# The causal mask and V's column sums go from TensorE to VectorE in a two-stage attention kernel

## The chip, the cores and the metric

The kernel runs on one core of a Trainium2 chip, as one program. The metric is the device time of one execution in microseconds (us). Several executions were timed, and one more was taken by the hardware profiler; the trace of that one is read below. The engines are PE (TensorE, matrix products), DVE (VectorE), ACT (ScalarE), POOL (GpSimd) and SP (SyncE, which issues the DMAs). PEld stands for the loading of PE's weights, the operand that stays in the array.

## The reference

Two stages. The first is attention of 8 heads in which a query sees only the keys that fall into the same hash bucket; the second is a mixture of 4 experts, each an attention with a causal mask, of which every token takes the best two.

```python
# first stage: batch 4, heads 8, sequence 768, head 64, 6 bits
q_bucket = np.sum((q @ proj > 0) * powers, axis=-1)      # k_bucket in the same way
mask = q_bucket[:, :, :, None] == k_bucket[:, :, None, :]
scores = np.where(mask, scale * q @ k.T, -1e9)
attn = softmax(scores)
x = attn @ v                                              # heads side by side: 512 columns

# second stage: 4 experts
logits = x @ w_gate                                       # the best two of four, softmax of these
scores = scale * (x @ wq[e]) @ (x @ wk[e]).T
scores = np.where(causal, -1e9, scores)                   # above the diagonal
out += gate * softmax(scores) @ (x @ wv[e]) @ wo[e]
```

(Shortened; `softmax` stands for the subtraction of the maximum, the exponential and the division.)

## The kernel before

**Units.** The work falls into 32 units of the first stage, ("L", batch, head), and 16 of the second, ("M", batch, expert). The list `seq` interleaves them: the experts of one batch stand between the heads of the next, and the last batch's experts come at the end. Heads are handled in pairs, and there are 16 pairs. The head with an even number is the first of its pair.

**A unit.** `max_steps` computes the scores once for their row maxima on DVE. `shift_steps` turns those into a row that is added through the product. `s_unit` then computes the scores a second time, transposed, in 6 chunks of 512 columns or fewer (`L_S`, `M_S`), in three steps for each chunk, `qk`, `lo` and `av`:

- `qk`: two matmuls of half-precision parts into one bank of PSUM (the accumulators that PE writes and DVE and ACT can read), then two exponentials on ACT, `p` in fp32 and `ph` in fp16. In an "M" unit a block on the diagonal gets a third matmul between the two, `ident16` against `mask_t`, which adds a large negative number above the diagonal. A unit has 6 such blocks, in 5 of its chunks.
- `lo`: POOL forms `pl`, the difference of `p` and `ph`.
- `av`: for each block of 128 queries and 128 keys three matmuls with `ph` or `pl` as the weights and 64 or 65 columns of `vh` or `vl` (V's high and low half) as the moving operand. The 65th column holds ones, so that the denominator comes along. `av` runs four to five chunks behind `qk`.

At the end of an "L" unit six matmuls of `vs` add a term with the sums of V's columns, and `normalise` divides.

**V.** `prep_v` prepares a pair: ACT writes V scaled as `vf` (fp32) and `vh` (fp16), POOL the difference `vl`. Each is one tile for the pair, with a column of ones at its outer sides: the first head's slice starts at element 1 and its denominator comes first (`first=1`, `den=0`), the second head's starts at element 66. Then PE sums V over all keys: 12 matmuls with one moving column (`ones`), which leave the sums as a column; a copy to `vcol`; a transpose on PE with `vcol` as weights; a copy and a subtraction to `vr`, two half-precision rows; and a DMA into `vs`:

```python
for n in range(2 * NT):
    x = vl[:, n // 2].rearrange("p h d -> p (h d)") if n % 2 else vh[:, n // 2, 2:2 + 2 * D]
    nc.tensor.matmul(p[:, 0:1], x, ones[:, 0:1], start=not n, stop=n == 2 * NT - 1)
```

**What sets the order.** Nothing is issued as it is written. A recorder (`Recorder`) collects every operation, and `schedule` lays them out on the engines, each engine in a fixed order. It goes by the table `TIMES` (what an operation costs by engine, operands and size), by a priority for each job (its place in the program plus the entry of the table `PLACE` for that job and engine), and by what is free: 8 PSUM banks, of which scores take up to 3 for `qk` (`st`), 2 for maxima (`mx`), 1 for the product with V (`o`) and 2 for the rest (`misc`). Copies out of PSUM may go to ACT or to DVE as the times fall (`copy`). In the first microseconds matmuls with `ident` fill PE's holes. Every operation has the one line L777 in the profile, where `issue` makes it, so names of tiles tell operations apart: `bank` is any bank of PSUM.

Of the kernel before, what the change touches and what calls it, by code (L numbers as in the profile page):

```python
# [134 lines left out]
class Op:  # L135
# [96 lines left out]
sync wo_l fr 768 773 701 1090 -400 0  # L232
gpsimd memset one - 2 1 SS 104 175 0 0 0
# [557 lines left out]
SHARED = 5  # L791
WHOLE = (4,)
# [26 lines left out]
def tile_kernel(ctx, tc, q, k, v, proj, wqk, wvg, wo, out):  # L819
# [71 lines left out]
    nc.gpsimd.memset(ones, 2.0 ** -10)  # L891

# [68 lines left out]
    FQ = [con.tile([128, S], HF, name=f"fq{i}") for i in range(2)]  # L961
    FQ.append(wo_l.rearrange("p t m -> p (t m)")[:, 0:S])
# [20 lines left out]
    for t in VR:  # L983
        nc.gpsimd.memset(t, 0.0)
        nc.gpsimd.memset(t[:, 0, 0:2], S / 1024.0)
        nc.gpsimd.memset(t[:, 0, 130:132], S / 1024.0)
    for t in VH + VF:
        nc.gpsimd.memset(t[:, :, 0:2], 1.0)
        nc.gpsimd.memset(t[:, :, 130:132], 1.0)
# [8 lines left out]
    wo_h = con.tile([128, EP, Dm], HF, name="wo_h")  # L998
# [286 lines left out]
    def prep_v(b, hp):  # L1285
# [13 lines left out]
        for h in range(2):  # L1299
            cv = vf[:, :, 2 + D * h:2 + D * h + D]  # L1300
            nc.scalar.activation(cv, nat[:, h].rearrange("p (j d) -> p j d", j=NT), AF.Copy, scale=c)
            hv = vh[:, :, 2 + D * h:2 + D * h + D]
            nc.scalar.activation(hv, cv, AF.Copy)
            nc.gpsimd.tensor_tensor(vl[:, :, h], cv, hv, op=OP.subtract)
            if not h:
                yield 0
        for h in range(2):
            w = slice(1 + 65 * h, 66 + 65 * h)
            U["L", b, 2 * hp + h].update(vf=vf[:, :, w], vh=vh[:, :, w], vl=vl[:, :, h], first=1 - h, den=64 * h,
                                         order=[2 * (i % 3) + i // 3 for i in range(NT)], c=c, vs=vs.rearrange("p h d -> p (h d)")[:, w])  # L1310
        yield 0
        p = misc()
        for n in range(2 * NT):
            x = vl[:, n // 2].rearrange("p h d -> p (h d)") if n % 2 else vh[:, n // 2, 2:2 + 2 * D]
            nc.tensor.matmul(p[:, 0:1], x, ones[:, 0:1], start=not n, stop=n == 2 * NT - 1)
        col = sb.tile([128, 1], FT, name="vcol")
        nc.copy(col, p[:, 0:1])
        nc.tensor.transpose(p[0:1, 128:256], col, ident)
        vr = VR[(npair[0] - 1) % NV]
        nc.copy(vr[:, 0, 2:2 + 2 * D], p[0:1, 128:256])  # L1320
# [116 lines left out]
    def s_unit(u):  # L1437
# [11 lines left out]
        def qk(c):  # L1449
            def f():  # L1450
                p = psum.tile([128, 512], FT, name="st", bufs=3)
                o = 0
                for j, q0, q1 in chunks[c]:
# [4 lines left out]
                    if diag:  # L1458
                        nc.tensor.matmul(p[:, o:o + 128], ident16, mask_t, start=False, stop=False)
# [514 lines left out]
```

## Time and profile before

| | us |
|---|---|
| median of 3 runs | 603.07 (602.51 to 603.36) |
| the profiled execution | 602.15 |
| its span, first to last instruction | 600.2 |
| PE busy | 587.3 (98%) |
| ACT busy | 502.4 (84%) |
| DVE busy | 493.3 (82%) |
| POOL busy | 471.3 (79%) |
| PE's weight loads busy | 429.2 (72%) |

The granted clock of PE is 0.998 of full speed over the span. Matmuls overlap: the time of one runs from its start to the modelled end of its result, while the next one starts long before that. What a matmul keeps PE from is read from start to start.

### The profile page before, as it was taken

How to read it: one execution, taken by the hardware profiler on the slowest of the kernel's cores; microseconds unless marked ns; L12 is line 12 of the kernel's file. 1: busy time of each engine (PE TensorE's matmuls, PEld its weight loads, DVE VectorE, ACT ScalarE, POOL GpSimd, SP SyncE). 2: the span in 40 equal slices, each digit the busy share in tenths (PEclk: the TensorE clock that was granted, in tenths of full speed). 3: DMA queues.
4: the chain of work that ended last, by engine and by line, in shares of the span. 5: the costliest groups of instructions: out<-in, count | busy, mean ns of one | idle time of the engine just before them, and what ended most of it. 6: DMA issues, size and time to landing. Idle time of an engine off the chain costs nothing.

```text
span 600.2 us, 20646 instructions
## 1 busy us (share of the span) xinstructions
PE 587.3 (98%) x7908; PEld 429.2 (72%) x7908; DVE 493.3 (82%) x1363; ACT 502.4 (84%) x1082; POOL 471.3 (79%) x527
## 2 busy tenths in 40 slices
PE   8999999999999999999999999999999999999996
PEld 7677776777777777777757676777667677767673
DVE  5998999999799898969868799987994886647843
ACT  6589999999799988897879897977879897954593
POOL 9479999898698998796967988977868797943291
PEclk9999999999999999999999999999999999999999
DMA  5563153241313223140341413240241111011212
GB/s 182 152 185 99 36 169 109 51 156 35 119 44 99 70 92 75 39 129 3 114 124 57 138 29 116 67 132 4 86 135 56 43 46 29 3 47 28 89 54 106
DMA packets 32920, 50.26 MB, mean 84 GB/s; under 512 B 6410, under 2 KB 20534, under 8 KB 32822
## 3 DMA queue, kind: packets, MB, share of 16 engines
q1 hardware_dynamic: 32810, 48.95, 28.1%
q8 instruction: 62, 1.02, 0.7%
q14 instruction: 36, 0.29, 0.2%
q10 hardware_dynamic: 12, 0.00, 0.0%
HBM read 20.98 MB, written 6.29 MB: 45 GB/s over the span
## 4 chain that ended last, share of the span: by engine, by line
PE 83%; ACT 7%; DVE 4%; issue 3%; POOL 2%; DMA 1%; POOLq 0%; ACTq 0%; DVEq 0%
PE bank L777 83%; ACT ph L777 3%; ACT p L777 2%; POOL pl L777 2%; DVE pmw L777 1%; DVE qk L777 1%; DMA xt<-roww 1%; ACT qk L777 0%; POOL vl L777 0%; DVE xt L777 0%; ACT vf L777 0%; DVE bank L777 0%; ACT wst L777 0%; DVE mw L777 0%; DVE pm L777 0%
## 5 line engine op out<-in xcount | busy, mean ns | idle before, releaser
L777 POOL TENSOR_TENSOR pl<-p,ph 128x512 f16<-128x512 f32 (+1 forms) x373 | 415.7, 1142 | 108.5 <-PE bank L777 57.4
L777 PE MATMUL bank<-qk 128*128 128x512 f16 (+13 forms) x1464 | 318.1, 323 | 0.7 <-DMA qk<-roww 0.5
L777 ACT ACTIVATE p<-bank 128x512 f32<-128x512 f32 x376 | 235.6, 632 | 22.4 <-PE bank L777 19.6
L777 ACT ACTIVATE ph<-bank 128x512 f16<-128x512 f32 x376 | 236.2, 637 | 2.8 <-PE bank L777 2.8
L777 DVE TENSOR_REDUCE pm<-bank 128x2 f32<-128x512 f32 (+2 forms) x284 | 184.1, 672 | 13.2 <-PE bank L777 12.7
L777 PEld LDWEIGHTS <-ph 128*128 128x128 f16 x2912 | 165.6, 98 | 25.9 <-issue 1.7
L777 PEld LDWEIGHTS <-qk 128*128 128x128 f16 (+5 forms) x1560 | 128.8, 98 | 47.4 <-issue 2.9
L777 PEld LDWEIGHTS <-pl 128*128 128x128 f16 x1456 | 134.9, 97 | 17.9 <-POOL pl L777 9.1
L777 PE MATMUL bank<-vh,pl 128*128 128x65 f16 x1120 | 135.7, 194 | 1.9 <-POOL pl L777 1.6
L777 PE MATMUL bank<-vl,ph 128*128 128x64 f16 x1120 | 136.3, 192 | 0.0
L777 PE MATMUL bank<-vh,ph 128*128 128x65 f16 x1120 | 136.1, 195 | 0.2
L777 PE MATMUL bank<-xt,wqk_h 128*128 128x384 f16 x256 | 56.0, 326 | 0.0
L777 DVE CUSTOM_DVE_ANT_0 spare<-bank,causal 128x512 bf16<-128x512 f32 (+2 forms) x96 | 44.1, 460 | 4.6 <-PE bank L777 2.9
L777 PE MATMUL bank<-mvh,pl 128*128 128x65 f16 x336 | 39.0, 193 | 0.5 <-POOL pl L777 0.4
L777 PE MATMUL bank<-mvh,ph 128*128 128x65 f16 x336 | 39.4, 194 | 0.0
L777 PE MATMUL bank<-mvl,ph 128*128 128x64 f16 x336 | 39.4, 192 | 0.0
L777 PEld LDWEIGHTS <-xt 128*128 128x128 f16 x324 | 30.2, 97 | 10.9 <-ACT xt L777 0.5
L777 PEld LDWEIGHTS <-wqk_h 128*128 128x128 f16 x256 | 24.1, 97 | 13.6 <-issue 0.3
L777 POOL TENSOR_TENSOR vl<-vf,vh 128x384 f16<-128x384 f32 x32 | 30.1, 951 | 3.6 <-ACT vh L777 1.7
L777 ACT ACTIVATE qk<-bank 128x384 f16<-128x384 f32 x29 | 14.2, 491 | 20.2 <-PE bank L777 19.8
L777 PE MATMUL bank<-wvg_h,xt 128*128 128x260 f16 x192 | 30.6, 274 | 0.0
L777 PE MATMUL bank<-xt,wqk_l 128*128 128x384 f16 x128 | 28.7, 326 | 0.0
(192 smaller groups left out, 862.1 us busy)
## 6 DMA issues: line engine op xcount, KB each, us to landing
qk<-qk SPq DMA_DIRECT2D x128, 96.0 KB
natv<-in_v_dram SPq DMA_DIRECT2D x16, 384.0 KB
qk<-qk SPq DMA_DIRECT2D x32, 192.0 KB
natq<-in_q_dram SPq DMA_DIRECT2D x15, 384.0 KB
natk<-in_k_dram SPq DMA_DIRECT2D x15, 384.0 KB
out_dram<-ot SPq DMA_DIRECT2D x20, 256.0 KB
wst<-in_wqk_dram SPq DMA_DIRECT2D x4, 256.0 KB
xt<-xt SPq DMA_DIRECT2D x4, 192.0 KB
```

Source lines behind the costliest of these rows:

```text
L777: o.made = getattr(getattr(self.nc, e), m)(*[real(x) for x in args], **{k: real(x) for k, x in kw.items()})
```

## The change

Five things.

- In batches three and four (`DMB = 2`) the mask matmul goes. In its place DVE adds `mask_t` to the diagonal blocks of the finished scores in PSUM, one instruction for a chunk, before the two exponentials. A chunk with two diagonal blocks gets one instruction over both.
- The sums of V: DVE reduces `vf` over the key blocks to `vsum`, and one fp32 matmul with a column of constants (`onef`) as weights gives the row of sums at once. The 12 matmuls, `vcol` and the transpose go.
- V's slices: in `vh`, `vf`, `vs` and `vr` the ones stand behind the first head's columns in place of before them. Slices start at elements 0 and 66, and `first` and `den` go.
- The three matmuls of a block in `av` are issued as `ph` with `vh`, `pl` with `vh`, `ph` with `vl`; before, the last two stood the other way round.
- `wo_h` (weights of the last product) is allocated earlier and lends its memory to one of the constant rows `FQ`, to make room. `PLACE` has new numbers throughout, and `TIMES` has entries for the new operations.

```diff
 PLACE = [
-    -2340, -66, -2158, -3742, 130, -1484, -2346, 0, -378, 2664, 594, -22, 1009, 7069, -1117, 0, -1213, 0, -496, -5437, 407, -4, -1918, 0,
...
+    -3968, -12221, -4294, 0, 0, -3011, 1476, -10216, -3028, 1347, 0, -672, -3509, -16, -851, -3, 291, -2773, -6556, 0, 25, 0, 0, 0,
...
+tensor matmul dt.float32 128 misc - 215 400 0 0 0
+vector tensor_reduce vsum vf 128 768 SS 870 950 0 0 0
...
+vector tensor_tensor st st 128 128 PP 235 260 0 0 0
+vector tensor_tensor st st 256 256 PP 370 395 0 0 0
...
+DMB = 2
...
+    onef = con.tile([128, 1], FT, name="onef")
+    nc.gpsimd.memset(onef, 2.0 ** -10)
...
-    FQ = [con.tile([128, S], HF, name=f"fq{i}") for i in range(2)]
-    FQ.append(wo_l.rearrange("p t m -> p (t m)")[:, 0:S])
+    wo_h = con.tile([128, EP, Dm], HF, name="wo_h")
+    FQ = [con.tile([128, S], HF, name="fq0")] + [x.rearrange("p t m -> p (t m)")[:, 0:S] for x in (wo_h, wo_l)]
...
     for t in VH + VF:
-        nc.gpsimd.memset(t[:, :, 0:2], 1.0)
+        nc.gpsimd.memset(t[:, :, D:D + 2], 1.0)
         nc.gpsimd.memset(t[:, :, 130:132], 1.0)
...
-            cv = vf[:, :, 2 + D * h:2 + D * h + D]
+            cv = vf[:, :, 66 * h:66 * h + D]
             nc.scalar.activation(cv, nat[:, h].rearrange("p (j d) -> p j d", j=NT), AF.Copy, scale=c)
-            hv = vh[:, :, 2 + D * h:2 + D * h + D]
+            hv = vh[:, :, 66 * h:66 * h + D]
...
-            w = slice(1 + 65 * h, 66 + 65 * h)
-            U["L", b, 2 * hp + h].update(vf=vf[:, :, w], vh=vh[:, :, w], vl=vl[:, :, h], first=1 - h, den=64 * h,
+            w = slice(66 * h, 66 * h + 65)
+            U["L", b, 2 * hp + h].update(vf=vf[:, :, w], vh=vh[:, :, w], vl=vl[:, :, h],
...
-        for n in range(2 * NT):
-            x = vl[:, n // 2].rearrange("p h d -> p (h d)") if n % 2 else vh[:, n // 2, 2:2 + 2 * D]
-            nc.tensor.matmul(p[:, 0:1], x, ones[:, 0:1], start=not n, stop=n == 2 * NT - 1)
-        col = sb.tile([128, 1], FT, name="vcol")
-        nc.copy(col, p[:, 0:1])
-        nc.tensor.transpose(p[0:1, 128:256], col, ident)
+        sums = sb.tile([128, 2, D], FT, name="vsum", bufs=1)
+        nc.vector.tensor_reduce(sums, vf.rearrange("p j (h c) -> p h c j", h=2)[:, :, 0:D], axis=AX.X, op=OP.add)
+        nc.tensor.matmul(p[0:1, 128:256], onef, sums.rearrange("p h d -> p (h d)"), start=True, stop=True)
...
-        nc.copy(vr[:, 0, 2:2 + 2 * D], p[0:1, 128:256])
-        nc.vector.tensor_tensor(vr[:, 1, 2:2 + 2 * D], p[0:1, 128:256], vr[:, 0, 2:2 + 2 * D], op=OP.subtract)
+        nc.copy(r0, row)
+        nc.vector.tensor_tensor(r1, row, r0, op=OP.subtract)
...
-                    if diag:
+                    if diag and u[1] < DMB:
                         nc.tensor.matmul(p[:, o:o + 128], ident16, mask_t, start=False, stop=False)
                     nc.tensor.matmul(p[:, o:o + w], d["kb"][:, ks], d["qb"][:, q0:q1], start=False, stop=True)
                     o += w
+                at, o1 = [], 0
+                for j, q0, q1 in chunks[c]:
+                    if not lsh and u[1] >= DMB and q0 == j * 128:
+                        at.append(o1)
+                    o1 += q1 - q0
+                if at:
+                    x = [p.rearrange("p (a b) -> p a b", b=128)[:, at[0] // 128:at[-1] // 128 + 1:max(1, (at[-1] - at[0]) // 128)] for _ in range(2)]
+                    nc.vector.tensor_tensor(x[0], x[1], mask_t[:, None, :].to_broadcast([128, len(at), 128]), op=OP.add)
...
-                        nc.tensor.matmul(ol, ph[:, o:o + 128], d["vl"][:, d["order"][j], 0:64], start=False, stop=False,
+                        nc.tensor.matmul(oa, pl[:, o:o + 128], d["vh"][:, d["order"][j], 0:65], start=False, stop=False,
                                          skip_group_check=True)
-                        nc.tensor.matmul(oa, pl[:, o:o + 128], d["vh"][:, d["order"][j], 0:65], start=False, stop=last and not lsh,
+                        nc.tensor.matmul(ol, ph[:, o:o + 128], d["vl"][:, d["order"][j], 0:64], start=False, stop=last and not lsh,
                                          skip_group_check=True)
```

Where the program's instructions stand, engine by engine. PE, before, the first two chunks' scores of unit ("M", 2, 0); `bank_10940` holds the first chunk:

```order
L777 MATMUL bank_10940<-qk 128x512
L777 LDWEIGHTS ident_80
L777 MATMUL bank_10940<-mask_t,ident_80 128x128
L777 LDWEIGHTS qk
L777 MATMUL bank_10940<-qk 128x512
L777 LDWEIGHTS qk
L777 MATMUL bank_10946<-qk 128x256
```

PE, after, the same place; `bank_10801` holds the first chunk:

```order
L785 MATMUL bank_10801<-qk 128x512
L785 LDWEIGHTS qk
L785 MATMUL bank_10801<-qk 128x512
L785 LDWEIGHTS qk
L785 MATMUL bank_10805<-qk 128x256
```

The mask's weights and matmul are gone from between the two products. DVE, after, the same unit; `bank_10839` is the chunk with two diagonal blocks, `ot` is the output of an earlier batch:

```order
L785 TENSOR_SCALAR ot<-bank_10753,xs 128x512
L785 TENSOR_TENSOR bank_10801<-bank_10801,mask_t 128x128
L785 TENSOR_TENSOR bank_10839<-bank_10839,mask_t 128x2x128
L785 CAST vr_239<-bank_10850 1x2x64
L785 TENSOR_TENSOR bank_10846<-bank_10846,mask_t 128x128
L785 TENSOR_TENSOR vr_239<-bank_10850,vr_239 1x2x64
L785 CAST row<-bank_10756 24x128
```

Three of the unit's five adds stand close together here, behind a copy of the output and among the sums of V and the shift of another unit. DVE, after, the third pair's sums of V, among row maxima (`pm`) and a maximum over weights (`qkmax`):

```order
L785 TENSOR_REDUCE pm_220<-bank_1348 128x2
L785 TENSOR_REDUCE pm_220<-bank_1371 128x2
L785 TENSOR_REDUCE qkmax<-wst 128x2
L785 TENSOR_REDUCE vsum<-vf_257 128x128
L785 TENSOR_SCALAR rden<-bank_1218,cs_563 128x6
L785 TENSOR_REDUCE mw<-qkmax 128x2
L785 TENSOR_REDUCE pm_220<-bank_1404 128x2
```

The reduction stands at place 117 of DVE's list; before, no instruction of DVE stood for it there. In all, PE's list goes from 7,864 matmuls to 7,629 and DVE's from 1,365 instructions to 1,418.

## Rows read from the trace of the kernel before

**Rows 1.** Page, part 1: busy us, share of the span, number of instructions.

```profile
PE 587.3 (98%) x7908; PEld 429.2 (72%) x7908; DVE 493.3 (82%) x1363; ACT 502.4 (84%) x1082; POOL 471.3 (79%) x527
```

**Rows 2.** Timeline of PE (start, us, instruction): 62 matmuls of an even head, 63 of an expert.

```profile
506.02 0.19 PE L777 MATMUL bank<-vh,ph 128*128 128x65 f16 x1
...
507.93 0.38 PE L777 MATMUL bank<-qk 78*128 78x512 f16 x1
...
545.53 0.19 PE L777 MATMUL bank<-mvh,ph 128*128 128x65 f16 x1
...
547.42 0.22 PE L777 MATMUL bank<-identh,negh 128*128 128x128 f16 x1
```

**Rows 3.** Busy time (and count) by stretch: PE, PEld, DVE, ACT, POOL; clock; DMA.

```profile
0.00:20.00 20.00, 17.55 (x214) 14.63 (x215) 11.58 (x21) 10.71 (x27) 16.53 (x95) 1.00 0.62 176
20.00:60.00 40.00, 37.64 (x466) 29.18 (x465) 36.89 (x89) 33.78 (x72) 30.96 (x29) 1.00 0.48 144
60.00:120.00 60.00, 58.91 (x838) 43.94 (x838) 59.11 (x142) 58.42 (x126) 54.37 (x51) 1.00 0.33 91
120.00:480.00 360.00, 357.91 (x4973) 259.69 (x4972) 309.70 (x868) 316.22 (x680) 297.64 (x281) 1.00 0.28 82
480.00:560.00 80.00, 79.90 (x1025) 58.78 (x1022) 53.58 (x173) 58.54 (x128) 55.70 (x58) 1.00 0.13 31
560.00:600.00 40.00, 35.35 (x405) 23.01 (x402) 22.43 (x74) 24.69 (x53) 16.12 (x16) 0.98 0.26 90
```

**Rows 4.** Waits: who for whom, us in total, times, the longest.

```profile
PEld L777 <- POOL pl L777: 9.1, 29, 0.8
```

**Rows 5.** Timeline of PE: a transpose, two mask matmuls, unit (2, 0)'s first product.

```profile
238.69 0.27 PE L777 MATMUL bank<-ident,vcol 128*1 128x128 f32 x1
238.80 0.19 PE L777 MATMUL bank<-vl,ph 128*128 128x64 f16 x1
238.83 0.22 PE L777 MATMUL bank<-mask_t,ident 128*128 128x128 bf16 x1
238.88 0.19 PE L777 MATMUL bank<-vh,pl 128*128 128x65 f16 x1
...
458.56 0.22 PE L777 MATMUL bank<-mask_t,ident 128*128 128x128 bf16 x1
458.62 0.38 PE L777 MATMUL bank<-qk 128*128 128x512 f16 x1
...
463.48 0.19 PE L777 MATMUL bank<-mvh,ph 128*128 128x65 f16 x1
```

**Rows 6.** Groups of DVE: shapes, count, busy us, mean ns of one, idle before.

```profile
L777 DVE CUSTOM_DVE_ANT_0 spare<-bank,causal 128x256 bf16<-128x256 f32 x48 | 19.9, 415 | 2.0 <-PE bank L777 1.3
...
L777 DVE TENSOR_REDUCE mqk<-natv 128x1 bf16<-128x768 f32 x14 | 13.2, 943 | 0.0
...
L777 DVE CUSTOM_DVE_ANT_0 spare<-bank,causal 128x128 bf16<-128x128 f32 x16 | 4.5, 281 | 0.3 <-PE bank L777 0.3
...
L777 DVE TENSOR_TENSOR bank<-bank,lg 128x96 f32<-128x96 f32 x8 | 2.1, 265 | 0.2
```

**Rows 7.** The chain that ended last: start, us, what; around the last unit.

```profile
559.91 24.40 PE bank L777 x294
...
584.35 0.84 ACT p L777
```

**Rows 8.** Timeline of PE: the first of nine one-column matmuls, and what follows the ninth.

```profile
481.75 0.16 PE L777 MATMUL bank<-ones,vl 128*128 128x1 f16 x1
...
481.98 0.38 PE L777 MATMUL bank<-qk 78*128 78x512 f16 x1
```

**Rows 9.** Timeline of PE: fp32 products of 384 columns, four side by side.

```profile
21.69 0.51 PE L777 MATMUL bank<-natq,pbd 128*32 128x384 f32 x1
...
22.03 0.49 PE L777 MATMUL bank<-natq,pbd 128*32 128x384 f32 x1
...
22.47 0.23 PE L777 MATMUL bank<-ident 128*128 128x128 bf16 x1
```

More of the change, by code (lines that the diff above doesn't have):

```diff
@@ L232 @@
 sync wo_l fr 768 773 701 1090 -400 0
+tensor matmul dt.float32 128 misc - 215 400 0 0 0
+vector tensor_reduce vsum vf 128 768 SS 870 950 0 0 0
+gpsimd memset onef - 1 1 SS 49 99 0 0 0
+gpsimd memset wo_h - 768 1 SS 674 727 0 0 0
+sync wo_h fr 768 773 701 1090 -400 0
+vector tensor_tensor st st 128 128 PP 235 260 0 0 0
+vector tensor_tensor st st 256 256 PP 370 395 0 0 0
 gpsimd memset one - 2 1 SS 104 175 0 0 0
@@ L984, in tile_kernel @@
         nc.gpsimd.memset(t, 0.0)
-        nc.gpsimd.memset(t[:, 0, 0:2], S / 1024.0)
+        nc.gpsimd.memset(t[:, 0, D:D + 2], S / 1024.0)
         nc.gpsimd.memset(t[:, 0, 130:132], S / 1024.0)
     for t in VH + VF:
-        nc.gpsimd.memset(t[:, :, 0:2], 1.0)
+        nc.gpsimd.memset(t[:, :, D:D + 2], 1.0)
         nc.gpsimd.memset(t[:, :, 130:132], 1.0)
@@ L997, in tile_kernel @@
     wvg_l = con.tile([128, KT, E * D + E], HF, name="wvg_l")
-    wo_h = con.tile([128, EP, Dm], HF, name="wo_h")
     causal = con.tile([128, 512], FT, name="causal")
@@ L1312, in prep_v @@
         p = misc()
-        for n in range(2 * NT):
-            x = vl[:, n // 2].rearrange("p h d -> p (h d)") if n % 2 else vh[:, n // 2, 2:2 + 2 * D]
-            nc.tensor.matmul(p[:, 0:1], x, ones[:, 0:1], start=not n, stop=n == 2 * NT - 1)
-        col = sb.tile([128, 1], FT, name="vcol")
-        nc.copy(col, p[:, 0:1])
-        nc.tensor.transpose(p[0:1, 128:256], col, ident)
+        sums = sb.tile([128, 2, D], FT, name="vsum", bufs=1)
+        nc.vector.tensor_reduce(sums, vf.rearrange("p j (h c) -> p h c j", h=2)[:, :, 0:D], axis=AX.X, op=OP.add)
+        nc.tensor.matmul(p[0:1, 128:256], onef, sums.rearrange("p h d -> p (h d)"), start=True, stop=True)
         vr = VR[(npair[0] - 1) % NV]
-        nc.copy(vr[:, 0, 2:2 + 2 * D], p[0:1, 128:256])
-        nc.vector.tensor_tensor(vr[:, 1, 2:2 + 2 * D], p[0:1, 128:256], vr[:, 0, 2:2 + 2 * D], op=OP.subtract)
+        r0, r1 = (vr[:, i].rearrange("p (h c) -> p h c", h=2)[:, :, 0:D] for i in range(2))
+        row = p[0:1, 128:256].rearrange("p (h d) -> p h d", h=2)
+        nc.copy(r0, row)
+        nc.vector.tensor_tensor(r1, row, r0, op=OP.subtract)
         nc.sync.dma_start(vs[FR0:FR0 + 2].rearrange("p h d -> p (h d)"), vr)
```

77 rows, old and new, of the table PLACE are left out of this document.

## The prediction

> **What bounds the kernel now.** I read the engine totals first, then the steps of single matmuls on the timeline, then the busy time by stretch, and last the waits. TensorE (PE) is busy 98% of the span, with 600.2 us of span against 587.3 us busy [rows 1]. Busy time alone proves little, because matmuls overlap, so the steps from start to start count: in unbroken work on attention weights times V, 62 matmuls of 64 or 65 columns go from 506.02 to 507.93 us and 63 from 545.53 to 547.42 us [rows 2], 30 ns each, and none of these waits. By stretch [rows 3], PE idles 2.45 us in the first 20 us, 2.4 us from 20 to 60, and 4.65 us in the last 40; between 60 and 560 us only 3.3 us of 500 (1.09, 2.09 and 0.10 in its three rows). PE's weight loads wait 9.1 us in all for `pl`, in 29 places [rows 4]; that is the longest wait of PE's that the view lists for an operand. So a matmul taken off PE is worth its step, at least after 120 us. One stretch is double bound: from 60 to 120 us VectorE (DVE) is busy 59.11 us and ScalarE 58.42 of 60 [rows 3].
>
> **The change, part by part.**
>
> Masks. 48 of the 96 mask matmuls go: 8 units (batches three and four, four experts each) with 6 diagonal blocks. From a mask matmul's start to the next one's it takes 0.05 us at 238.83 and 0.06 us at 458.56 [rows 5]: 48 x 0.055 = 2.6 us of PE. DVE gets 32 adds of 128 columns and 8 of 256 (one chunk per unit holds two diagonals). No row has this add; the nearest are a DVE add of 96 columns from PSUM to PSUM, 265 ns, and the custom add-and-maximum with a causal tile, 281 ns for 128 columns and 415 for 256 [rows 6]. I take the custom one, which also reads PSUM and SBUF: 32 x 0.281 + 8 x 0.415 = 12.3 us. DVE has room where most of them fall: after 480 us it is busy 53.58 of 80 and 22.43 of 40 us [rows 3].
> The add is a new wait between the scores and ScalarE's two exponentials, and behind those stand GpSimd's subtraction and PE's product with V. Behind the add on DVE's list stand maxima and normalisations. What hides it is the lead: in expert unit (2, 0) the first chunk's mask is at 458.56 us and its product with V at 463.48 us [rows 5], 4.9 us. An add of 0.3 us behind one other DVE instruction (0.94 us for the longest of [rows 6]) fits in. In the last unit nothing hides it, since the chain that ends last goes from PE at 584.31 us straight to ScalarE's `p` at 584.35 [rows 7]: one add of 0.28 us and a second handover of 0.04, or some more: I put it at 0.4 us.
>
> V's sums. For each of 16 pairs of heads, 12 matmuls with one column and a transpose go, and one fp32 matmul of 128 columns comes. The one-column ones step by 0.0256 us (481.75 to 481.98, nine steps [rows 8]): 192 x 0.0256 = 4.9 us. The transposes take 0.11 us from 238.69 to 238.80 [rows 5]: 16 x 0.11 = 1.8 us. The new matmul has a bound on either side. It could be as cheap as that fp32 transpose of the same 128 columns, 0.11 us. Or it costs what an fp32 product does: those of 384 columns run in two records, the second 0.34 us after the first, with the next matmul at 0.78 us [rows 9], so a third of 0.78 is 0.26 and a third of twice 0.34 is 0.23. It is an fp32 product and no transpose, so I take 0.23: 16 x 0.23 = 3.7 us. Net 4.9 + 1.8 - 3.7 = 3.0 us of PE; 4.9 at the cheap end and 2.5 at the dear one.
> The Trainium skill, "FP8 and Floating Point Precision", section "TensorE Precision Notes", says that true fp32 makes four passes through the array; four times 128 columns at 2.4 GHz is 0.213 us as an estimate from that page (the granted clock is 1.00 in [rows 3]), which would make the net 3.3 us and the time 597.2. The two records of [rows 9] fit it better than the transpose does.
> DVE pays for it: 16 reductions over 768 elements, each 943 ns by the reduction of `natv` [rows 6], so 15.1 us, less nine small copies of `vcol` that it had. After 120 us there is room for it. In the stretch from 60 to 120 us there is not: DVE started 21 + 89 instructions before it and 142 in it [rows 3], and the changed list has sums of V at its places 117, 147 and 225. That is 2.8 us more against some 0.9 us of idle time; ScalarE, which can take copies over, has 1.6. So it costs between nothing and 1.9 us; I take 1.0.
>
> V's even slices. In the even heads `vh` and `vf` were read from an odd element and the product with `vl` was written one column further; now all start at even places. A triple of matmuls (high-high, high-low, low-high) takes 1.91 / 62 x 3 = 92.4 ns in an even head and 1.89 / 63 x 3 = 90.0 ns in an expert unit [rows 2], whose slices are even already. With 16 even heads of 36 blocks and 2.4 ns each that is 576 x 2.4 = 1.4 us. If neither the odd start nor the shifted column is its cause, it is 0.
>
> The order inside a triple becomes high-high, low-high, high-low. With 10 ns steps no row shows which of the three carries the odd nanoseconds, so I bound it by the difference above, 2.4 ns in either direction on all 1,456 triples (32 x 36 + 16 x 21, less the 32 blocks that the first eight units take in fp32): 3.5 us. I take 0: the columns and the operands are the same. `pl` is wanted one matmul earlier, 29 waits x 0.03 us, below 0.9 us and inside that bound.
>
> What is hidden. `wo_h` lends its memory to a constant row of the first units in place of `fq`; its weights are written later than those units read it. The DMA count is 394 before and after, and the small row of sums goes out in one DMA as before. PE's list up to the first product with V has the same matmuls but for a few fillers, so the first 30 us should stay. Later every list is in another order, and nothing in it has a price of its own: I leave it at the stated margins.
>
> **The sum.** 2.6 + 3.0 + 1.4 = 7.0 us leave PE; 1.0 us is lost from 60 to 120 us and 0.4 us at the end: 5.6 us. The profiled execution took 602.15 us, 1.95 more than its span and 0.92 below the median of 603.07, so 596.55 for it and 597.5 for the median.
>
> **The rivals.**
>
> The new order in a triple pays: 3.5 us more, 597.5 - 3.5 = 594.0. For it speaks that a triple's 65 + 64 + 65 columns at 2.4 GHz are 80.8 ns of the 90.0 that it takes, so something beside columns costs time; against it that three matmuls with the same operands stay, and no row shows that their order matters.
>
> DVE binds early. In the first 120 us PE waits on others anyway, so the first six pairs' sums (6 x 0.19 = 1.1 us) and four even heads (0.3 us) bring nothing, and the three reductions lengthen the stretch by the full 1.9: 7.0 - 1.4 - 1.9 - 0.4 = 3.3, so 599.8; with two more sums between 20 and 60 us on the path (DVE busy 36.89 of 40 [rows 3]) 601.7.
>
> PE is not the bound. Its weight loads are busy only 72% [rows 1], and if operands, not matmuls, set the pace, each matmul removed leaves a hole: 603.1, or 603.5 with the last unit's add. Steps at 30 ns without a wait speak against it. The Trainium skill, "Perfetto Trace Analysis", section "Identifying the Most-Contended Engine", calls matmul busy time a bad measure of headroom and points to the share of weight loads; by that rule a quarter of PE would be free. The waits of [rows 4] do not agree.
>
> Slower: the adds stand on the path of each masked chunk. Then 12.3 us of adds pass to PE, and 603.07 - 7.0 + 12.3 = 608.4. It decides once DVE's queue eats the 4.9 us lead, or where units follow each other with less lead, as at the end. Against it: DVE is idle a third of the time from 480 to 560 us and 44% after that [rows 3].
>
> **How the numbers follow.** My forecast has 0.55, the triple's order 0.15, DVE early 0.16, PE not the bound 0.06, slower 0.08. A measurement of this kernel can tell about 0.2%, 1.2 us, from no change. Faster by more than that: 0.55 + 0.15 + 0.14 of DVE's 0.16 = 0.84; within: 0.02 + 0.06 = 0.08; slower 0.08. The range goes from the triple's gain with no loss early (593.0) to the far end of DVE early (601.8), and leaves out about 0.16 and some of the lower tail.
>
> **What would show it.** Right: 48 mask matmuls, 40 DVE adds near 0.28 and 0.41 us; the V matmul in two records 0.11 us apart; triples of even heads at 90 ns; PE idle after 120 us as small as now; PE's busy time lower by about 7 us. Wrong: adds waited for by `p` for whole microseconds and PE waiting on `pl` far over 9 us; a stretch from 60 to 120 us that takes 2 us or more longer for the same units; triples unchanged at 92 ns, or all of them faster.

## The result and the profile after

The changed kernel takes 604.80 us (median of 21 runs, 602.64 to 611.03) where the kernel before takes 602.25 us beside it (21 runs): the ratio is 1.0055, 95% interval 1.0039 to 1.0071. It is slower by half a per cent. I had forecast 597.5 us and a range up to 601.8, so the sign is wrong, and the time lies above the range. In 9 of the 21 executions PE's granted clock was 0.991 to 0.994 over the span, and they took 606.6 to 611.0 us; the other 12, at 0.998 or more (full clock below), have a median of 604.0.

The engine totals of after, which answer to [rows 1]:

```profile
PE 584.2 (97%) x7689; PEld 420.9 (70%) x7689; DVE 521.3 (87%) x1416; ACT 500.4 (83%) x1068; POOL 474.6 (79%) x529
```

TensorE (PE) is busy 3.1 us less, not 7.0. Its span grew from 600.2 to 602.3 us, so it now stands idle 18.1 us instead of 12.9: 5.2 us more, where I had put 1.4. The first error is 3.9 us, the second 3.8, and together they are the 7.7 us between a forecast gain of 5.6 and a loss of 2.1 in the profiled execution. VectorE (DVE) is busy 28.0 us more.

Busy time by stretch of after, with the columns of [rows 3]:

```profile
0.00:20.00 20.00, 17.52 (x220) 15.04 (x220) 12.39 (x23) 10.71 (x27) 16.51 (x96) 1.00 0.59 164
20.00:60.00 40.00, 37.14 (x432) 28.74 (x432) 39.44 (x87) 33.47 (x71) 31.22 (x30) 1.00 0.57 160
60.00:120.00 60.00, 56.67 (x795) 41.90 (x794) 58.67 (x145) 58.09 (x117) 53.56 (x48) 1.00 0.30 81
120.00:480.00 360.00, 356.09 (x4823) 254.01 (x4821) 320.10 (x877) 314.33 (x672) 297.32 (x280) 1.00 0.29 81
480.00:560.00 80.00, 79.41 (x1002) 57.08 (x1003) 62.15 (x192) 56.36 (x126) 56.02 (x58) 1.00 0.15 36
```

PE's idle time in the last four of these rows is 2.86, 3.33, 3.91 and 0.59 us, where it was 2.36, 1.09, 2.09 and 0.10. DVE is now full from 20 us on (39.44 of 40), not only from 60.

The groups of DVE that the change adds, and the one by which I priced the first, of after (columns as in [rows 6]):

```profile
L785 DVE TENSOR_REDUCE vsum<-vf 128x128 f32<-128x768 f32 x16 | 25.0, 1563 | 0.4 <-ACT vf L785 0.3
...
L785 DVE TENSOR_REDUCE mqk<-natv 128x1 bf16<-128x768 f32 x14 | 13.1, 939 | 0.0
...
L785 DVE TENSOR_TENSOR bank<-bank,mask_t 128x128 f32<-128x128 f32 x32 | 9.2, 294 | 2.7 <-PE bank L785 1.9 <-ACT ph L785 0.4
...
L785 DVE TENSOR_TENSOR bank<-bank,mask_t 128x256 f32<-128x256 f32 x8 | 3.4, 424 | 2.1 <-PE bank L785 2.1
```

The mask additions came at 294 and 424 ns, forecast 281 and 415. The reductions of V came at 1,563 ns, forecast 943: as many elements are read as for `natv`, but it takes 0.62 us longer.

The fp32 product of V's sums on PE's timeline of after, with the work on either side (columns as in [rows 2]):

```profile
176.94 0.60 PE L785 MATMUL bank<-qk 78*128 78x256 f16 x4
177.47 0.38 PE L785 MATMUL bank<-vsum,onef 128*1 128x128 f32 x2
177.78 0.39 PE L785 MATMUL bank<-qk 78*128 78x512 f16 x1
```

Its two records are 0.11 us apart, as I had said, but the next matmul starts 0.31 us after the first of them. The four matmuls ahead of it take 0.53 us, and four of this shape take 0.44 us where something else follows (below). So the product costs 0.40 us, not 0.23.

Three of PE's four longest waits of after (who waits for whom, us in total, times, the longest; the fourth, 1.9 us for `ident`, is there in the kernel before too, with 1.8):

```profile
PE bank L785 <- POOL pl L785: 2.9, 8, 0.6
...
PE bank L785 <- DVE vsum L785: 1.5, 3, 0.7
PE bank L785 <- DVE rden L785: 0.9, 1, 0.9
```

The waits of weight loads for `pl`, which were 9.1 us [rows 4], are 8.4. What I had feared most, exponentials behind the mask additions, is there (ScalarE's `p` waits 5.5 us for them in 8 places) but PE does not show it as a wait.

### The profile page after: what moved, and what is told of

It reads as the page before. It is cut to its first block, busy times and chain, and to the rows that moved or that the text cites. A ratio compares the mean times of both kernels' runs of the same rounds, so it can differ in the third digit from the quotient of the medians.

```text
span 602.3 us, 20254 instructions
## 1 busy us (share of the span) xinstructions
PE 584.2 (97%) x7689; PEld 420.9 (70%) x7689; DVE 521.3 (87%) x1416; ACT 500.4 (83%) x1068; POOL 474.6 (79%) x529
## 4 chain that ended last, share of the span: by engine, by line
PE 64%; DVE 14%; ACT 13%; issue 4%; POOL 2%; DMA 2%; ACTq 0%; SPq 0%; POOLq 0%; DVEq 0%
PE bank L785 64%; ACT ph L785 5%; ACT p L785 5%; DVE pm L785 4%; POOL pl L785 2%; DVE vsum L785 2%; DVE qk L785 1%; DVE pmw L785 1%; DVE bank L785 1%; DVE xt L785 1%; ACT qk L785 1%; DMA qk<-M 1%; DMA xt<-roww 1%; DVE mqk L785 1%; ACT xt L785 0%
## 5 line engine op out<-in xcount | busy, mean ns | idle before, releaser
L785 POOL TENSOR_TENSOR pl<-p,ph 128x512 f16<-128x512 f32 x374 | 419.5, 1149 | 104.9 <-ACT ph L785 48.8
L785 PE MATMUL bank<-qk 128*128 128x256 f16 (+15 forms) x1464 | 311.9, 324 | 3.7 <-DVE rden L785 0.9
L785 ACT ACTIVATE p<-bank 128x512 f32<-128x512 f32 x376 | 230.7, 616 | 40.7 <-PE bank L785 30.4
L785 ACT ACTIVATE ph<-bank 128x512 f16<-128x512 f32 x376 | 231.3, 620 | 0.2 <-PE bank L785 0.2
L785 PEld LDWEIGHTS <-ph 128*128 128x128 f16 x2912 | 159.1, 97 | 16.7 <-issue 1.2
L785 PEld LDWEIGHTS <-qk 128*128 128x128 f16 (+5 forms) x1560 | 127.1, 98 | 58.4 <-issue 7.4
L785 PEld LDWEIGHTS <-pl 128*128 128x128 f16 x1456 | 133.1, 97 | 22.6 <-POOL pl L785 8.4
L785 PE MATMUL bank<-vh,pl 128*128 128x65 f16 x1120 | 126.1, 194 | 3.3 <-POOL pl L785 2.9
L785 PE MATMUL bank<-vh,ph 128*128 128x65 f16 x1120 | 126.1, 193 | 0.1
L785 PE MATMUL bank<-vl,ph 128*128 128x64 f16 x1120 | 125.0, 192 | 0.0
```

Source lines behind the costliest of these rows:

```text
L785: o.made = getattr(getattr(self.nc, e), m)(*[real(x) for x in args], **{k: real(x) for k, x in kw.items()})
```

## The experiments

Three theories stood against each other. **Load**: DVE's new work comes where it has no time to spare. **Product**: the product of V's sums makes PE pay 0.17 us more than I had put. **Order**: the parts are worth what the sum says, and the new order of all lists loses it. Times below are medians; ratios are to the kernel before, run in the same set.

**The change in the old order.** In e1 all parts but the new order are done: each new instruction stands where the first of those that it replaces stood. e2 has the product with 128 columns of weights besides; e3 is the changed kernel with that edit alone; e4 is the kernel before with V's even slices alone, its sums running over columns that stand two further along. Edits here and below are shortened; `...` and `<...>` stand for what is left out or told in words.

```
e1, e2: order of the kernel before; even slices, VectorE's sums, VectorE's mask additions
e2, e3: -onef = con.tile([128, 1], FT, name="onef")
        +onef = con.tile([128, 128], FT, name="onef")
        -nc.tensor.matmul(p[0:1, 128:256], onef, sums...)
        +nc.tensor.matmul(p[:, 128:256], onef, sums...)
e4:     -w = slice(1 + 65 * h, 66 + 65 * h)
        +w = slice(66 * h, 66 * h + 65)
```

> Every part of the change but one: the even slices, VectorE's 16 sums of V with the fp32 product behind each, VectorE's 24 mask additions, the shared buffer; all instructions stand in the order of the kernel before (nothing is placed anew, each new instruction stands where the first of those it replaces stood). Theory order (the parts are worth what the sum says, and the new order of the instructions loses it): the change's gain shows, 1 to 3 us under the kernel before (599 to 601 where before is 602.2). Theory load (VectorE's 28 us more come at places where it has none to spare, and it is late whatever the order): at or over the kernel before, 602 to 606. Theory product (the fp32 product costs TensorE 0.40 us, not 0.23): no bound on the whole, but TensorE's steps around each of the 16 products sum to 0.4 us as in the changed kernel.

> As the first kernel of this set, but the fp32 product of V's sums has 128 columns of weights (and writes 128 partitions, of which one is read) instead of 1. Theory product (a one-column product runs in another shape of the array than its neighbours, and TensorE pays about 0.09 us on the way in and 0.09 us on the way out): the steps around each product fall from 0.40 to 0.2 to 0.25 us, TensorE is busy 2.5 to 3 us less, and the time is 1 to 3 us under that of the first kernel of this set. Rival (the 0.40 us are the fp32 passes themselves or a wait on VectorE's row): the steps stay at 0.4 us and the two kernels agree within 0.5 us.

> The changed kernel with its own order, its fp32 product of V's sums with 128 columns of weights instead of 1. Theory product: TensorE busy 581.5 instead of 584.2 us, the time 1.5 to 3 us under the changed kernel, 601.8 to 603.3. Theory order or theory load (the loss is in waits between 51 and 140 us): at most 1 us less than the changed kernel, 603.8 to 604.8, and the 4.7 us lost between the units that end at 51 and at 93 us stay.

> The kernel before with V's slices on even starts alone; order and instruction count as before (the sums of V run over columns that stand two further along, so part of them is wrong; it is the same work). Theory even (each triple of an even head takes 2.4 to 2.5 ns less, 576 of them): TensorE busy 1.4 us less, time 600.5 to 601.2 where before is 602.2. Rival (the waits take it back, since the same order meets the same late tiles): 602.0 to 602.4, with TensorE's busy time down all the same.

Measured: e1 620.22 us (1.0309, 1.0267 to 1.0350), e2 618.55 us (1.0274, 1.0245 to 1.0304), e3 604.44 us (1.0034, 1.0015 to 1.0053), e4 601.37 us (0.9986, 0.9971 to 1.0001).

The theory of order falls in the form that I gave it: in the old order the change (with 40 mask additions, not the 24 of my text on e1) loses 18 us, so the new order, with the places that it gives to the new instructions, wins most of that back. Other places for them in the old order were not tried. Unit by unit, e2 is 11.3 us behind the kernel before when the fourth head of the fourth batch ends (at 462 us there), the last unit ahead of the first whose masks moved, and loses 4.7 us more after that. Up to there DVE's new work is the sums alone; the last part has all the mask additions and one of the sums (at 495 us), so what the masks cost in it is not shown. Of PE's waits in e2 those for DVE's maxima and the sums come first:

```profile
PE bank L779 <- DVE pm L779: 4.8, 6, 1.5
PE bank L779 <- DVE vsum L779: 4.7, 5, 1.3
PE bank L779 <- POOL pl L779: 3.6, 9, 0.8
```

The theory of the product holds for its price. In e3 the same place reads:

```profile
176.14 0.60 PE L785 MATMUL bank<-qk 78*128 78x256 f16 x4
176.58 0.38 PE L785 MATMUL bank<-vsum,onef 128*128 128x128 f32 x2
176.80 0.38 PE L785 MATMUL bank<-qk 78*128 78x512 f16 x1
```

With 128 columns of weights the product takes 0.22 us and the four matmuls ahead of it 0.44: 0.09 us less on either side, 16 x 0.18 = 2.9 us if every place were like this one. Why one column costs this is open: the transpose of [rows 5] has one column too and 0.11 us to the next matmul. PE's busy time fell by 2.4 us, as expected:

```profile
PE 581.8 (97%) x7689; PEld 424.0 (71%) x7689; DVE 521.3 (87%) x1416; ACT 500.5 (83%) x1068; POOL 475.0 (79%) x529
```

How much of it the time follows is not settled. By the two ratios it is 0.2% less, inside their intervals; the six of e3's twelve executions at full clock have a median of 602.9 us, 1.1 under the changed kernel's 604.0; the profiled one has a span of 600.1 us, 2.2 under, with PE idle as long as in the changed kernel (18.3 us). The even slices alone gave 1.5 us of PE's busy time (585.8) and 0.8 us of time, at the edge of what can be told.

**DVE's load taken away.** All four keep the order of the changed kernel.

```
e5: -nc.vector.tensor_reduce(sums, <six blocks of keys of vf, 132 elements apart>, ...)
    +nc.vector.tensor_reduce(sums, <one block of keys of vf>, ...)
e6: +nc.vector.tensor_reduce(sums, <six neighbouring elements of vf>, ...)
e7: -nc.vector.tensor_tensor(x[0], x[1], mask_t..., op=OP.add)
    +nc.tensor.matmul(p[:, o:o + 128], ident16, mask_t, start=False, stop=False)
e8: e5, and no mask in the third and fourth batch, and 128 columns of weights
```

> The changed kernel, its order too, but each of VectorE's 16 reductions of V reads one block of keys instead of six (128 elements of a partition instead of 768): the sums of V leave five blocks of six out. It takes VectorE's time for the sums away and leaves every instruction and every wait in place. Theory load (the reductions measure 1.563 us and not the 0.94 that my sum had; the three that stand between 60 and 120 us, and the one or two ahead of them, are what is lost there, since VectorE has no idle time in that stage): each falls to some 0.3 us, 20 us less of VectorE, the 3.4 us lost between the units that end at 51 and at 93 us shrink to under 1, and the time is 600 to 602. Theory order (the instructions as they stand now lose it, whatever the reductions take): 603.5 to 605, and the loss between 51 and 93 us stays over 2.5 us.

> The changed kernel, but each reduction of V sums six neighbouring elements where the change sums six elements that stand 132 apart: as many read, as many written (the sums are of other elements, so they aren't those of V's rows). Theory stride (the 0.62 us by which a reduction is over that of natv, with as many elements read, come from reading 528 bytes apart): 0.94 to 1.0 us each, 10 us less of VectorE, and the time between the changed kernel and the one with short sums, 602 to 603.5. Rival (they come from 128 results of a partition where natv has one): 1.5 to 1.6 us each, and the time of the changed kernel, 604 to 605.

> The changed kernel with the masks of the third and fourth batch put back: TensorE's 48 mask matmuls stand in the places they had, VectorE's 40 additions are left out, all else stays. Theory mask pays (the additions lie beside other work, TensorE saves 2.6 us by them; units between 437 and 591 us gained 1.9 us on the kernel before): TensorE busy 2.6 us more, time 606 to 607.5. Theory load in its form for the late stages (exponentials wait for the additions, 5.5 us on ScalarE, and the tail pays): 603 to 604.5, no more than the changed kernel.

> The changed kernel and its order without VectorE's new work: short sums (one block of keys of six), no mask addition in the third and fourth batch (so no mask there), and 128 columns of weights in the fp32 product. It is what the change would be worth in this order if VectorE's part cost nothing. Theory load: TensorE's 5.5 us show in full, 596.5 to 598.5, my forecast. Theory order: the order by itself holds 2 us or more of waits over the kernel before, 599 to 601.

Measured: e5 601.24 us (0.9983, 0.9961 to 1.0004), e6 601.12 us (0.9985, 0.9969 to 1.0001), e7 606.14 us (1.0068, 1.0044 to 1.0093), e8 599.20 us (0.9943, 0.9924 to 0.9963).

So load is the larger part of the loss. In e6 only the addresses differ that the reductions read, and the kernel goes from 0.55% slower to 0.15% faster, some 4 us. (Its sums are not V's. So it is with e5, e8 and e10: they show what a part costs, and are no kernels to use.) The row of e6's reductions, and its totals:

```profile
L785 DVE TENSOR_REDUCE vsum<-vf 128x128 f32<-128x768 f32 x16 | 15.1, 943 | 0.4 <-ACT vf L785 0.4
...
PE 582.8 (97%) x7689; PEld 420.8 (70%) x7689; DVE 514.2 (86%) x1416; ACT 500.0 (84%) x1068; POOL 473.7 (79%) x529
```

It is my 943 ns to the nanosecond: 128 results instead of one cost nothing, the step of 132 elements (528 bytes) between the six that are summed costs 0.62 us. The Trainium skill, "SBUF — State Buffer", section "Door 1: The DMA port swizzle", says in a box that reads which leave a 16-byte line at each step pay a penalty, so that four fp32 elements are the most that can be strided for free; this agrees, and the page has no price for it. PE's busy time falls by 1.4 us too, with the same matmuls, so lateness counts in that total as well: of the 3.9 us above, 2.4 are the product's (e3) and 1.4 go with the long reductions.

e5, with 276 ns for a reduction, is no faster than e6, so at 943 ns the sums are already covered. But the place was not where I had said. Of the time that was lost between the ends of the second head (51 us) and the fifth (93 us), 4.6 us in the changed kernel (4.1 in e9, a second trace of it), 3.6 stays in e5 and 3.8 in e6; I had expected under 1. The rest of the gain comes later. Two rows of e6 by stretch:

```profile
60.00:120.00 60.00, 57.49 (x805) 42.74 (x804) 58.76 (x147) 59.15 (x120) 54.83 (x49) 1.00 0.29 81
120.00:480.00 360.00, 357.62 (x4865) 255.81 (x4863) 317.74 (x882) 316.69 (x677) 298.89 (x282) 1.00 0.29 81
```

PE's idle time falls from 3.33 to 2.51 us in the first and from 3.91 to 2.38 in the second (e9 has 2.96 and 3.58). So most of the wait, 1.2 to 1.5 us, lay in the 360 us where DVE had 40 us to spare and ten of the long reductions stood, and 0.4 to 0.8 us in the 60 where it had none and three stood. What an engine has to spare in a stretch doesn't say how soon an instruction behind a long one is wanted.

e7 puts 2.6 us back on PE (586.8 busy, as forecast) and is 1.3 us slower than the changed kernel by the medians and 1.8 by the spans (604.1 and 602.3), but the intervals overlap: the masks' part doesn't lose, and how much it pays is not settled. In e8, with 4.4 us left of DVE's new work, PE's busy time is 6.2 us under the kernel before and the gain is 3.4 us (0.57%), 2.2 us short of my 5.6. PE's idle time from 60 to 120 us is still there:

```profile
60.00:120.00 60.00, 57.47 (x805) 43.95 (x805) 56.75 (x147) 59.16 (x120) 54.87 (x49) 1.00 0.29 81
```

DVE is no longer full in it (56.75, with 59.11 before), so what these 2.5 us are over the 1.09 of before belongs to the order in which the work stands now. Two of e8's waits of PE in this stretch:

```profile
PE bank L785 <- POOL pl L785: 0.9, 2, 0.6
PE bank L785 <- DMA qk<-M: 0.8, 1, 0.8
```

The kernel before waits there for `pl` too (0.8 us) and for no such DMA. So 0.8 of the 1.4 us is one DMA that comes too late. ScalarE is full in this stretch (59.16 us, 58.42 before); whether that makes the rest was not tried.

**Both cures, and the order in a triple.** e9 is the changed kernel again, e10 has dense sums and wide weights, e11 gets the true sums by three additions (with wide weights), e12 puts back the order in a triple.

```
e11: -nc.vector.tensor_reduce(sums, <vf>, ...)
     +nc.vector.tensor_tensor(vp, <blocks 0, 1 of vf>, <blocks 2, 3>, op=OP.add)
     +nc.vector.tensor_tensor(vp, vp, <blocks 4, 5>, op=OP.add)
     +nc.vector.tensor_tensor(sums, vp[:, 0], vp[:, 1], op=OP.add)
e12:  nc.tensor.matmul(oa, ph, vh)
     -nc.tensor.matmul(oa, pl, vh)
      nc.tensor.matmul(ol, ph, vl)
     +nc.tensor.matmul(oa, pl, vh)
```

> The changed kernel itself, beside the three others of this set: its runs spread over 8 us, and kernels of other sets can be compared with it only by way of the kernel before. 604 to 605 by every theory.

> The changed kernel with both cures at once: reductions that read neighbouring elements (0.94 us instead of 1.56; the sums are of other elements than V's rows, as in e6) and 128 columns of weights in the fp32 product (0.22 us instead of 0.40). VectorE's mask additions stay. Theory load and product together (the two losses stand in different places and add up): 3.5 us for the first and 0.5 to 2.5 us for the second, 598.5 to 601, and TensorE's span full but for what the kernel before also waited. Rival (only one of the two binds, the other is taken back by waits): 600.8 to 601.5, the time of the dense sums alone.

> The changed kernel with each reduction replaced by three additions that give the same sums: blocks 0 and 1 plus blocks 2 and 3 (256 elements of a partition), plus blocks 4 and 5 (256), and the two halves (128), which by the trace's additions of 128x256 and 128x128 (0.42 and 0.29 us) take 1.13 us together and read runs of 64 neighbouring elements; and 128 columns of weights. It computes the whole function. Theory load and product: a little over the kernel with dense sums (0.2 us more each), 599 to 601.5, faster than the kernel before by 0.2 to 0.5%. Rival (strided reads of 64 elements are slow as well, or three instructions wait more than one): 602.5 to 604.5.

> The changed kernel with the two corrections of each triple in the order they had, all else in place (the product of the low probabilities comes last again). By the working on record the order within a triple costs nothing while its tiles are there, 0 within 3.5 us. Theory none: 604 to 605, the time of the changed kernel. Theory weights (two steps on one V slice behind each other save TensorE's time): over 606. Rival (the new order makes TensorE wait for the low probabilities one step earlier, 30 ns, in each of the 576 places): 0.5 us less at most.

Measured: e9 603.98 us (1.0050, 1.0027 to 1.0073), e10 599.09 us (0.9968, 0.9950 to 0.9986), e11 632.29 us (1.0532, 1.0491 to 1.0574), e12 605.08 us (1.0058, 1.0038 to 1.0079).

e10 is 0.82% under e9 of the same set: with both errors of my prices taken away, the change is 0.32% faster than the kernel before (1.9 us by the ratio, 2.8 by the medians, where the forecast was 5.6). It is 0.17% under e6, inside the intervals: here too about 1 us of the wide weights' 2.9 shows. e12 and e9 agree: the order in a triple is nothing that can be told.

e11 missed by 30 us. Its timeline, at a place where one addition has GpSimd beside it and the next has not:

```profile
431.64 1.35 POOL L785 TENSOR_TENSOR pl<-p,ph 128x512 f16<-128x512 f32 x1
...
432.00 1.26 DVE L785 TENSOR_TENSOR spare<-spare,vf 128x256 f32<-128x256 f32 x1
...
433.30 0.29 DVE L785 TENSOR_TENSOR vsum<-spare 128x128 f32<-128x128 f32 x1
```

The addition of 256 elements starts while GpSimd subtracts and ends 0.27 us after it, 1.26 us long. The one of 128 elements runs alone at my 0.29 us. Of the 16 of this last kind no other ran with GpSimd idle, and those 15 took 0.65 to 1.13 us, 1.05 on average. The groups of e11:

```profile
L785 DVE TENSOR_TENSOR spare<-spare,vf 128x256 f32<-128x256 f32 x16 | 18.5, 1154 | 0.6
...
L785 DVE TENSOR_TENSOR vsum<-spare 128x128 f32<-128x128 f32 x16 | 16.0, 1002 | 0.6
```

The rows by which I had priced them, the mask additions, read one operand from PSUM, and show nothing of this. The Trainium skill, "SBUF — State Buffer", section "SBUF: two separate sides", says that a DVE instruction with two SBUF inputs and a GpSimd instruction that reads SBUF shut each other out for a whole instruction; these durations agree.

Part of the 30 us comes by way of PE's clock. In e11's trace PE's granted clock is 0.50, the lower of its two levels (1.2 GHz, not 2.4), for 20 us in six places between 51 and 373 us, each behind a wait of PE for DVE of 1.5 to 2.2 us. The matmuls of 64 or 65 columns step by 54 ns there and by 29 elsewhere, so by an estimate from these numbers some 9 us are the clock's.

**The true sums at the dense price.** In e13 V's fp32 tile is turned, so that the six elements of a sum are neighbours, and the weights are wide.

```
-VF = [con.tile([128, NT, 132], FT, name=f"vf{i}") for i in range(NV)]
+VT = [con.tile([128, 132, NT], FT, name=f"vf{i}") for i in range(NV)]
+VF = [x.rearrange("p c j -> p j c") for x in VT]
```

> The changed kernel with V's fp32 tile turned: the six blocks of keys of one column stand side by side (24 bytes) and the columns behind each other, so that the reduction reads neighbouring elements and its sums are V's true sums; and 128 columns of weights in the fp32 product. All that is computed is the reference's. In turn ScalarE writes that tile, and ScalarE, GpSimd and TensorE's products of whole chunks read it, with a step of 24 bytes instead of 4. Theory load (VectorE is the engine that can't spare time; ScalarE and GpSimd can spare some): reductions 0.94 us, and the time of the kernel with dense sums and wide weights (599.1) if the strided accesses of the others cost little, up to 1.5 us more if ScalarE's 32 scaled copies (0.66 us) and GpSimd's 32 subtractions (0.92 us) grow by half: 598.5 to 601. Rival (the cost of the step only moves, and binds there): 602 to 606, with ScalarE or GpSimd waited for.

Measured: 610.02 us (1.0145, 1.0127 to 1.0163). The rival held in its mechanism, and the time lies above the 602 to 606 that it gave. DVE's reductions are at 945 ns, but two groups of ScalarE grew from 660 and 555 ns in the changed kernel to:

```profile
L785 ACT ACTIVATE vf<-natv,cs 128x384 f32<-128x384 f32 x32 | 31.8, 1037 | 0.0
...
L785 ACT ACTIVATE vh<-vf 128x384 f16<-128x384 f32 x32 | 29.6, 933 | 0.5 <-PE bank L785 0.5
```

That is 0.38 us for 384 elements written or read with a step of 24 bytes, 64 times, 24 us in all on an engine that was busy 58.09 of 60 us early on; PE then waits for its exponentials (0.2 us in the changed kernel):

```profile
PE bank L785 <- ACT ph L785: 5.1, 13, 1.0
```

The step's cost moved to an engine that could spare it less. None of the versions here with V's true sums is faster than the kernel before.

## Why the prediction was wrong, point by point

**What bounds the kernel: right for most of it, and read too simply.** PE's steps are the bound while its operands are there. I took idle time of DVE per stretch as room for more work on it; e1, e5 and e6 show that much of the room was spoken for.

**Masks: right on PE (2.6 us), and the additions' sizes were right.** Their worth in time, 1 to 2 us by e7, is not settled.

**V's sums: two terms mis-sized, and this decided the sign.** The fp32 product: I gave it 0.23 us and bounds of 0.11 and 0.26; it is 0.40 with 1 column of weights, which takes 2.7 us of the 3.0 that this part was to bring to PE. I had priced it by products with 32 columns of weights; the one row with one column, the transpose, pointed the other way, down to 0.11, and I took the two for the ends. The reduction: I gave it the 943 ns of `natv`, because the shape of the operand was the same; but that one reads neighbours, and this one steps 528 bytes, which the diff said in plain sight. With 1,563 ns it put 9.9 us more on DVE than the sum had, and e6 prices this at 4 us of the kernel's time.

**V's even slices: right.** Twelve triples of an even head in after, in the columns of [rows 2]:

```profile
175.86 0.19 PE L785 MATMUL bank<-vh,ph 128*128 128x65 f16 x1
...
176.94 0.60 PE L785 MATMUL bank<-qk 78*128 78x256 f16 x4
```

1.08 us for 36 matmuls is 90.0 ns a triple, where it was 92.4; e4 finds 1.5 us of busy time.

**The order in a triple: right at 0** (e12), and the bound of 3.5 us on it, with the rival that hung on it, was far too wide.

**The 1.0 us lost from 60 to 120 us:** 2.2 us there, and 2.8 us more idle time in the other stretches between 20 and 560, where I had none. This is the step that failed beside the two prices: I looked for DVE's limit only where it was full.

**The new order: left at the stated margins, wrongly.** Against the plain places of e1 it is worth some 15 us, and from 60 to 120 us it also leaves PE 1.4 us more idle time than before even when DVE has room (e8), 0.8 of it behind one DMA. With both prices put right (e10) 2.8 to 3.7 of the forecast 5.6 us are still missing; the part of them that is not in these waits stays open.

The rival that DVE binds early named the mechanism, but carried the same 943 ns, so it ended at 601.7 and not above 602. The slower rival, additions on the path of each masked chunk, did not happen.

## What to carry to other kernels

Price an instruction by a row with the same access pattern, not only the same shape: the step between the elements that it reads, whether both operands lie in SBUF, and how many columns of weights a matmul loads each changed a price here, by 66 to 245%. Work moved off the bounding engine has to be paid on another in time, not in busy share: look who stands behind the new instruction in its queue. And when an order has been fitted to a kernel, a part tried in another's order can come out far too badly (e1).

## What the runs showed of the hardware

An fp32 product with 1 column of weights between matmuls with 128 costs 0.09 us extra ahead of it and 0.09 us behind it (0.40 us against 0.22 with 128 columns), where PE does not wait. Reading fp32 with a step of 528 bytes makes a reduction of 768 elements on VectorE 1,563 ns instead of 943; a step of 24 bytes adds 0.38 us to 384 elements on ScalarE, written or read, and 0.2 us to GpSimd's subtraction (924 to 1,121 ns). Additions on VectorE with both operands in SBUF took 1.05 us on average beside GpSimd's work, and 0.29 alone (once), for 128 elements. At a granted clock of 0.50 matmuls of 64 or 65 columns step by 54 ns, at 1.00 by 29 (e11).
